# FFT filter and MLP on one Trainium2 core: first matmul two chunks ahead on a third PSUM bank, FFT steps in halves

## The chip, the cores and the metric

The kernel runs on 1 core of a Trainium2 chip. The metric is the device time in microseconds from start to end of one execution; several executions are made and their median counts.

## The reference

```python
X = np.fft.rfft(x, axis=1)                    # x: 8 images x 3008 tokens x 256
Y = X * (filt_r + 1j * filt_i)[None]
x = np.fft.irfft(Y, n=3008, axis=1).reshape(24064, 256)
h = x @ w_in                                  # 256 -> 2048
g = h * (1 / (1 + np.exp(-1.702 * h)))
out = g @ w_out                               # 2048 -> 256
```

All inputs are float32. The kernel gets the accuracy of float32 from pairs of matmuls on split numbers: a value is a high part (float32r) and a low part, and products of high x high, high x low and low x high are summed in PSUM.

## The kernel before, in words

**The work.** The 3008-point transform is split into 64 x 47 points. For each image (b = 0 to 7) it takes: stage one (64-point transforms over the rows of x, result a stored to DRAM as a_d), stage two (16 frequency groups: 47-point transform, product with the filter, inverse 47-point transform, result b stored to DRAM as b_d), and per tile of tokens the last inverse transform (`signal`, L626), which makes y. The MLP (`mlp`, L688) works on tiles of 512 tokens, six per image (384 for the sixth of an even image), 48 in all.

**The MLP.** A tile has 16 chunks of 128 hidden columns. `first(fc)` makes h with six matmuls (L701) into a bank of `ps_h` (two banks). ScalarE writes gh, the high part of the gelu (L704), and the gelu itself back into the bank (L705); VectorE subtracts and writes gl (L706), which frees the bank. `second(fc)` adds gh and gl times w_out into two banks of `ps_o` (L723), six matmuls; the two of gl are held over to the next chunk. The loop at the end of the program goes through all chunks: `ahead` calls `first` of chunk n + 1, then comes `second` of chunk n.

**The FFT beside it.** While the MLP works on image b, the generator `fft(b + 1)` (L448) makes the transform of the next image. It yields between steps. A planner in the main loop (L787, L808) gives each step a cost (`COSTS`, L25) and runs it when the tokens passed reach the matching share of `whole`:

```python
passed, whole = 0, sum(widths) - (40 if b else 26)
while steps and spent + steps[0] <= sum(COSTS[b]) * passed / whole + 0.01:
    run(nxt, 1)
```

For images 2 to 7 stage one is `packed` (L483): `fetch` loads x two blocks ahead (SP's queue), `butterfly` adds and subtracts on GpSimd (L504), `split` casts the high part on ScalarE or VectorE (L511) and subtracts on GpSimd (L512), `transform` (L514) does two matmuls (L521) into two banks of `ps_f` (four banks), casts the high parts (L526: h = 0 on ScalarE, h = 1 on VectorE) and on VectorE subtracts and adds (L527, L528). The two stores of each of the 12 transforms go into the list `late`; `keep` issues them from ScalarE's queue one step later (L453). Image 1 uses `thrice`, image 0 a function of its own ahead of the loop.

Stage two: `load` fetches from a_d by GpSimd's queue (L558), `forward` (L579) does the matmuls of both halves k into two banks (`second`, L569 to L574; tile s), merges them (`halves`, L442 on ScalarE, L443 on VectorE), multiplies with the filter (L433 to L436) and splits the product into y (tile zy, L590 on VectorE, L591 on GpSimd). `backward` (L597) transforms that back (tile i), merges it and stores b from ScalarE's queue (L606). Each forward step is followed by the backward step of the group before.

**What sets the order.** Tile's scheduler orders each engine's instructions by a forecast of its own, with program order as the priority, and may issue an instruction well ahead of its place in the program. `keep_in_program_order` pins an instruction behind what was traced on its engine before; the first matmul of each FFT step is pinned. Engines run their queues in order. `signal` of the next tile is started at the chunks in `at` (L811): loads of br, then the two halves of the last transform (L674, L682, L683).

Of the kernel before, what the change touches and what calls it, by code (L numbers as in the profile page):

```python
# [19 lines left out]
NH = 24  # L20
P = 128
Q = 112
NFC = DFF // P
LATER = [1.0, 1.4] + [1.25, 0.75] * 15 + [1.0]
COSTS = [[0.746] * 12 + [1.212] * 2 + LATER] + [[0.8] * 3 + [1.35] * 12 + [1.3] * 2 + LATER] * 7  # L25

# [132 lines left out]
def tile_kernel(  # L159
# [13 lines left out]
    dram1 = ctx.enter_context(tc.tile_pool(name="dram1", bufs=1, space=bass.MemoryType.DRAM))  # L173
    ps_f = ctx.enter_context(tc.tile_pool(name="ps_f", bufs=4, space=bass.MemoryType.PSUM))
    ps_h = ctx.enter_context(tc.tile_pool(name="ps_h", bufs=2, space=bass.MemoryType.PSUM))
# [5 lines left out]
    def half(name):  # L181
        return sb.tile([P, 2, D], F32R, tag="half", name=name, bufs=5)

    in_order = [True]
# [107 lines left out]
    def bank(name):  # L292

        pool, tag = banks[n_bank[0] % 4]
        n_bank[0] += 1
        return pool.tile([P, 2, D], F32, tag=tag, name=name)

# [139 lines left out]

    def halves(ps, dst):

        for k in range(2):  # L440
            h, o = slice(64 * k, 64 * k + 48), slice(64 - 64 * k, 112 - 64 * k)
            nc.scalar.copy(dst[h], ps[k][o])  # L442
            nc.vector.tensor_tensor(dst[h], ps[k][h], dst[h], ALU.add)  # L443

    def fft(b):
# [10 lines left out]
        def thrice():  # L456

            for c in range(6):
# [3 lines left out]
                for u in range(2):  # L462
                    xh, xl = half(f"xh_{b}_{c}_{u}"), half(f"xl_{b}_{c}_{u}")
                    src = xr[:, 2 * u : 2 * u + 2, :]
                    nc.scalar.copy(xh, src)
                    nc.gpsimd.tensor_tensor(xl, src, xh.bitcast(F32), ALU.subtract)
                    ps = ps_f.tile([P, 2, D], F32, tag="f", name=f"s1_{b}_{c}_{u}")
                    mm3(ps, t1_sb[0][:, 0], t1_sb[0][:, 1], xh, xl)
                    su = slice(2 * u, 2 * u + 2)
                    nc.scalar.copy(ah[:, su], ps)  # L470
                    nc.vector.tensor_tensor(al[:, su], ps, ah[:, su].bitcast(F32), ALU.subtract)
                    keep()
                    yield
# [9 lines left out]
        def packed():  # L483
# [21 lines left out]

            def split(n):
                if n < 12:
                    src = sums.pop(n)
                    es[n] = [half(f"e{h}_{b}_{n}") for h in range(2)]
                    for h, (t, o) in enumerate(sides):  # L510
                        (nc.vector.tensor_copy if h else nc.scalar.copy)(es[n][h][t], src[t])  # L511
                        nc.gpsimd.tensor_tensor(es[n][h][o], src[t], es[n][h][t].bitcast(F32), ALU.subtract)  # L512

            def transform(n):  # L514
                c, j = divmod(n, 2)
                a = sb.tile([P, 2, 2, D], F32, tag="raw", name=f"a_{b}_{n}", bufs=7)
                ps = [ps_f.tile([P, 2, D], F32, tag="f", name=f"s1_{b}_{n}_{h}") for h in range(2)]
                e = es.pop(n)
                for h in range(2):
                    w = t1_sb[1][:, h, j].rearrange("p a c -> p (a c)")  # L520
                    ins = nc.tensor.matmul(ps[h], w, e[h], start=True, stop=True)  # L521
                    if h == 0:
                        tc.keep_in_program_order(ins)
                for h, (t, o) in enumerate(sides):
                    hi, lo = a[t, 0].bitcast(F32R), a[t, 1]
                    (nc.vector.tensor_copy if h else nc.scalar.copy)(hi, ps[h][t])  # L526
                    nc.vector.tensor_tensor(lo, ps[h][t], a[t, 0], ALU.subtract)  # L527
                    nc.vector.tensor_tensor(lo.bitcast(F32R), lo, ps[h][o], ALU.add)  # L528
                    q = NH * j + 4 * c + 2 * h
                    to = a_d[:, :, q : q + 2].rearrange("k s n d -> s k n d")  # L530
                    late.append((to, a[t]))

            for c in range(2):
                fetch(c)
            yield
            butterfly(0)
            butterfly(1)
            yield
            split(0)
            yield  # L540
            for n in range(12):
                transform(n)
                split(n + 1)
                butterfly(n + 2)
                if n % 2 == 0:
                    fetch(n // 2 + 2)
                if n:
                    keep()
                yield

# [12 lines left out]

        def second(i, m, src, name):

            ps = [ps_f.tile([P, 2, D], F32, tag="f", name=f"{name}_{b}_{i}_{k}") for k in range(2)]
            for k in range(2):
                if i == 0:
                    ins = nc.tensor.matmul(ps[k][:, 0], de_sb[:, k, m + 1], src[:, k, 0], start=True, stop=True)  # L569
                    if k == 0:  # L570
                        tc.keep_in_program_order(ins)
                    nc.tensor.matmul(ps[k][:, 1], de_sb[:, k, m], src[:, k, 1], start=True, stop=True)
                else:
                    ins = nc.tensor.matmul(ps[k], de_sb[:, k, m], src[:, k], start=True, stop=True)  # L574
                    if k == 0:
                        tc.keep_in_program_order(ins)
            return ps

        def forward(i):  # L579

            ps = second(i, 0, zy[0][:, i % 2], "s2")
            if i + 2 < 16:
                load(i + 2)
            u1 = c_buf[i % 3]
            halves(ps, u1)
            product(i, u1, u1, f_buf[:Q, 2 * (i % 2) : 2 * (i % 2) + 2])
            y = zy[0][:, 2 + i % 2]
            for k in range(2):
                h, o = slice(64 * k, 64 * k + 48), slice(64 - 64 * k, 112 - 64 * k)
                nc.vector.tensor_copy(y[h, k], u1[h])  # L590
                nc.gpsimd.tensor_tensor(y[o, k], u1[h], y[h, k].bitcast(F32), ALU.subtract)  # L591
            if i + 2 < 16:
                load_f(i + 2)

        bes = {}

        def backward(i):  # L597
            g, u = divmod(i, 2)
            if u == 0:
                bes[g] = raw(f"b_{b}_{g}")  # L600
            ps = second(i, 2, zy[0][:, 2 + i % 2], "i2")
            halves(ps, bes[g][:Q, 2 * u : 2 * u + 2, :])
            if u == 1:
                be = bes.pop(g)
                for k in range(2):
                    nc.scalar.dma_start(b_d[:, 32 * k + 4 * g : 32 * k + 4 * g + 4, :], be[64 * k : 64 * k + 48])  # L606

# [9 lines left out]
        for i in range(17):  # L617
            if i < 16:
                forward(i)
                yield  # L620
            if i:
                backward(i - 1)
                yield
        b_of[b] = b_d

    def signal(b, t, y):  # L626
# [11 lines left out]
        def turn(m):  # L638

            ps = ps_f.tile([P, 4, P], F32, tag="f", name=f"bt_{t}_{m}")  # L640
            if t == m == 0:
# [25 lines left out]
        for m in range(2):  # L667
            if b == 0 and 1 not in br:
                br[1] = turn(1)
            ps = ps_f.tile([P, 512], F32, tag="f", name=f"i1_{b}_{t}_{m}")  # L670
            if b == t == m == 0:
# [15 lines left out]

    def mlp(b, t, y, nb, sums=(ps_o, "o")):  # L688

# [6 lines left out]
        def first(fc):  # L696
            ps = ps_h.tile([P, 512], F32, tag="h", name=f"h_{b}_{t}_{fc}")
            half, o = divmod(fc, HALF)
# [10 lines left out]
        def second(fc, hold):  # L709
            if fc == 0:  # L710
                pos.extend(sums[0].tile([P, 512], F32, tag=sums[1], name=f"o_{b}_{t}_{m}") for m in range(2))
            gp = gs.pop(fc)
# [61 lines left out]
    def ahead(i, fc):  # L774
        if i not in chunks_of:
            b, t = tiles[i]
            chunks_of[i] = mlp(b, t, ys.pop((b, t)), 4 if t < 5 or b % 2 else 3, (ps_f, "f") if i == 1 else (ps_o, "o"))
        chunks_of[i][0](fc)

    ahead(*turns[0])  # L780
    for n, (i, fc) in enumerate(turns):
        b, t = tiles[i]
        if n % (6 * NFC) == 0:

            lead = 16 if b == 0 else 0
            widths = [3 if k // NFC == 5 and b % 2 == 0 else 4 for k in range(lead, 6 * NFC)]
            passed, whole = 0, sum(widths) - (40 if b else 26)  # L787
            steps, spent = list(COSTS[b]), 0.0
            nxt = fft(b + 1) if b + 1 < B else iter(())
        if n == 0:  # L790
            run(start(*tiles[1]))
        if n + 1 < len(turns):
            ahead(*turns[n + 1])
        chunks_of[i][1](fc, turns[n + 1 : n + 2] == [(i, fc + 1)])
# [11 lines left out]
        if b or n >= lead:  # L806
            passed += widths.pop(0)
            while steps and spent + steps[0] <= sum(COSTS[b]) * passed / whole + 0.01:  # L808
                run(nxt, 1)
                spent += steps.pop(0)  # L810
        at = (9, 12, 13) if t == 5 else (1, 3, 9)  # L811
        if n in (23, 26, 27) or i > 1 and fc in at and i + 1 < len(tiles):
# [35 lines left out]
```

## Time and profile before

| | us |
|---|---|
| median of 3 runs | 2419.93 (2415.69 to 2422.02) |
| the profiled execution | 2423.5 |
| its span, first to last instruction | 2421.7 |

The rows below are of this one profiled execution. PE is TensorE's matmuls, PEld its weight loads, DVE VectorE, ACT ScalarE, POOL GpSimd, SP the queue of loads and output stores; "ACTq" is an instruction that ScalarE's sequencer issues. A number in square brackets at the end of a line of the timeline is the engine's idle time before it, and what ended it.

### The profile page before, as it was taken

How to read it: one execution, taken by the hardware profiler on the slowest of the kernel's cores; microseconds unless marked ns; L12 is line 12 of the kernel's file. 1: busy time of each engine (PE TensorE's matmuls, PEld its weight loads, DVE VectorE, ACT ScalarE, POOL GpSimd, SP SyncE). 2: the span in 40 equal slices, each digit the busy share in tenths (PEclk: the TensorE clock that was granted, in tenths of full speed). 3: DMA queues.
4: the chain of work that ended last, by engine and by line, in shares of the span. 5: the costliest groups of instructions: out<-in, count | busy, mean ns of one | idle time of the engine just before them, and what ended most of it. 6: DMA issues, size and time to landing. Idle time of an engine off the chain costs nothing. (4 is left out here: it accounts for less than half of the span.)

```text
span 2421.7 us, 31798 instructions
## 1 busy us (share of the span) xinstructions
PE 2371.3 (98%) x11030; PEld 1973.8 (82%) x11030; DVE 1653.3 (68%) x2561; ACT 1305.8 (54%) x2431; POOL 918.0 (38%) x819
## 2 busy tenths in 40 slices
PE   9999999999999999999999999999999999999999
PEld 7878897788777888788877788878887788898887
DVE  7968857788477883878848788387883878822222
ACT  6666655466444664456644466445664456644443
POOL 3035534355343552535525355253542535500000
PEclk9999999999999999999999999999999999999999
DMA  8265433455334552345524454244542445320000
GB/s 330 87 184 113 109 107 96 100 116 116 83 109 100 123 118 84 99 105 119 116 86 104 105 129 110 74 111 105 119 114 74 118 104 126 96 65 9 18 9 18
DMA packets 139952, 248.77 MB, mean 103 GB/s; under 512 B 15376, under 2 KB 81040, under 8 KB 139792
## 3 DMA queue, kind: packets, MB, share of 16 engines
q1 hardware_dynamic: 63088, 136.25, 19.2%
q0 software_dynamic: 46592, 44.05, 10.7%
q10 hardware_dynamic: 30112, 66.44, 10.6%
q8 instruction: 88, 1.44, 0.2%
q14 instruction: 72, 0.59, 0.1%
HBM read 152.83 MB, written 93.85 MB: 102 GB/s over the span
## 5 line engine op out<-in xcount | busy, mean ns | idle before, releaser
L701 PE MATMUL h<-y,wi 128*128 128x512 f32 (+1 forms) x4608 | 1172.8, 390 | 24.0 <-DVE gl L706 23.8
L701 PEld LDWEIGHTS h<-y,wi 128*128 128x128 f32 x4608 | 854.1, 189 | 202.4 <-DVE gl L706 44.5
L706 DVE TENSOR_TENSOR gl<-h,gh 128x512 fp32r<-128x512 f32 (+1 forms) x768 | 522.4, 680 | 571.6 <-ACT h L705 561.2
L704 ACT ACTIVATE gh<-h 128x512 fp32r<-128x512 f32 (+1 forms) x768 | 452.9, 590 | 819.4 <-PE h L701 625.6
L723 PE MATMUL o<-gh,wo 128*128 128x512 f32 (+1 forms) x3072 | 821.1, 387 | 14.7 <-ACT gh L704 14.7
L723 PEld LDWEIGHTS o<-gh,wo 128*128 128x128 f32 x3072 | 573.6, 189 | 127.9 <-ACT gh L704 18.9
L723 PE MATMUL o<-gl,wo 128*128 128x512 f32 (+1 forms) x1536 | 476.7, 387 | 3.2 <-DVE gl L706 3.2
L705 ACT ACTIVATE h<-h 128x512 f32<-128x512 f32 (+1 forms) x768 | 448.3, 584 | 0.0
L591 POOL TENSOR_TENSOR zy<-c_buf,zy 48x512 fp32r<-48x512 f32 x224 | 315.2, 1407 | 74.7 <-DVE zy L590 66.0
L723 PEld LDWEIGHTS o<-gl,wo 128*128 128x128 f32 x1536 | 288.7, 189 | 60.7 <-DVE gl L706 5.3
L436 POOL TENSOR_TENSOR c_buf<-c_buf,u_buf 112x512 f32<-112x512 f32 x127 | 163.9, 1290 | 388.4 <-DVE c_buf L435 388.4
L558 POOL DMA_DIRECT2D zy<-a_d x224 | 130.6, 588 | 223.8 <-DMA a_d<-a 113.5
L512 POOL TENSOR_TENSOR e<-ev,e 64x512 fp32r<-64x512 f32 x72 | 96.7, 1343 | 246.8 <-ACT e L511 228.3
L443 DVE TENSOR_TENSOR c_buf<-s,c_buf 48x512 f32<-48x512 f32 x224 | 154.3, 689 | 33.6 <-ACT c_buf L442 29.3
L443 DVE TENSOR_TENSOR b<-i,b 48x512 f32<-48x512 f32 x224 | 154.1, 688 | 15.0 <-ACT b L442 9.6
L442 ACT COPY c_buf<-s 48x512 f32<-48x512 f32 x224 | 130.3, 582 | 51.0 <-PE s L574 30.9
L442 ACT COPY b<-i 48x512 f32<-48x512 f32 x224 | 130.2, 581 | 48.6 <-PE i L574 42.1
L512 POOL TENSOR_TENSOR e<-x,e 64x512 fp32r<-64x512 f32 x72 | 92.8, 1289 | 64.5 <-ACT e L511 47.5
L590 DVE CAST zy<-c_buf 48x512 fp32r<-48x512 f32 x224 | 94.6, 422 | 32.9 <-POOL c_buf L436 26.9
L674 PEld LDWEIGHTS i<-tab,br 128*128 128x128 f32 x752 | 100.9, 191 | 8.8 <-PE s L521 1.2
L674 PE MATMUL i<-tab,br 128*128 128x128 f32 x752 | 103.0, 275 | 0.1
L527 DVE TENSOR_TENSOR a<-s,a 64x512 f32<-64x512 f32 x144 | 99.2, 689 | 4.4
(113 smaller groups left out, 1483.4 us busy)
## 6 DMA issues: line engine op xcount, KB each, us to landing
f_buf<-fs SPq DMA_DIRECT2D x224, 192.0 KB, 3.1
zy<-a_d POOLq DMA_DIRECT2D x224, 192.0 KB, 3.6
a_d<-a ACTq DMA_DIRECT2D x144, 256.0 KB, 3.1
x<-in_x_dram SPq DMA_DIRECT2D x47, 512.0 KB, 5.1
out_dram<-out SPq DMA_DIRECT2D x43, 512.0 KB, 3.9
b_d<-b ACTq DMA_DIRECT2D x112, 192.0 KB, 2.5
br<-b_d SPq DMA_DIRECT2D x84, 256.0 KB, 4.6
f_y<-in_filt_dram SPq DMA_DIRECT2D x8, 512.0 KB, 8.3
```

Source lines behind the costliest of these rows:

```text
L436: eng.tensor_tensor(u1, u1, u2, ALU.add)
L442: nc.scalar.copy(dst[h], ps[k][o])
L443: nc.vector.tensor_tensor(dst[h], ps[k][h], dst[h], ALU.add)
L512: nc.gpsimd.tensor_tensor(es[n][h][o], src[t], es[n][h][t].bitcast(F32), ALU.subtract)
L558: nc.gpsimd.dma_start(zy[0][64 * k : 64 * k + 48, i % 2].rearrange("p k s d -> p (k s) d"), src)
L591: nc.gpsimd.tensor_tensor(y[o, k], u1[h], y[h, k].bitcast(F32), ALU.subtract)
L674: ins = nc.tensor.matmul(ps[:, P * i : P * i + P], br[m][:, i], t2_sb, start=True, stop=True)
L701: nc.tensor.matmul(ps[:, :w], wi_sb[half][:, wk, kc, c], y[:, yk, kc, :w], start=n == 0, stop=n == 5)
L704: nc.scalar.activation(gh[:, :w], ps[:, :w], AF.Gelu_apprx_sigmoid)
L705: nc.scalar.activation(ps[:, :w], ps[:, :w], AF.Gelu_apprx_sigmoid)
L706: nc.vector.tensor_tensor(gl[:, :w], ps[:, :w], gh[:, :w].bitcast(F32), ALU.subtract)
L723: ins = nc.tensor.matmul(pos[m][:, :w], wb[:, P * m : P * m + P], g[:, :w], start=first_one, stop=last_one)
```

## The change

`ps_f` has three banks, and one bank `ps_x` is lent out by a new function `ring`. For images 1 to 7 it is the third bank of h. `first` runs two chunks ahead of `second` there. The functions `transform`, `split`, `forward` and `backward` do one half (h or k) per step with one bank; both high casts of `transform` are on ScalarE. A store is issued when more than two are in the list. There is one more empty step between the first fetch and the butterflies. The costs follow; `whole` is less by 48 instead of 40; `at` is earlier for images 1 to 7. The product of `forward` begins with half 0 while half 1 is still to come. Arithmetic and the number of instructions of each kind stay, apart from the engine of 72 casts. The core of the diff:

```diff
-LATER = [1.0, 1.4] + [1.25, 0.75] * 15 + [1.0]
-COSTS = [[0.746] * 12 + [1.212] * 2 + LATER] + [[0.8] * 3 + [1.35] * 12 + [1.3] * 2 + LATER] * 7
+LATER = [0.5, 0.5, 1.0, 0.4] + [0.625, 0.625, 0.375, 0.375] * 15 + [1.0]
+COSTS = [[0.746] * 12 + [1.212] * 2 + LATER] + [[0.8] * 4 + [0.675] * 24 + [1.3] * 2 + LATER] * 7
...
-    ps_f = ctx.enter_context(tc.tile_pool(name="ps_f", bufs=4, space=bass.MemoryType.PSUM))
+    ps_f = ctx.enter_context(tc.tile_pool(name="ps_f", bufs=3, space=bass.MemoryType.PSUM))
+    ps_x = ctx.enter_context(tc.tile_pool(name="ps_x", bufs=1, space=bass.MemoryType.PSUM))
...
+    shared, turn_of = ["f"], {"f": 0, "h": 0}
+
+    def ring(kind, shape, name):
+
+        own = {"f": (ps_f, 3), "h": (ps_h, 2)}[kind]
+        turn_of[kind] += 1
+        if shared[0] == kind and turn_of[kind] % (own[1] + 1) == 0:
+            return ps_x.tile(shape, F32, tag="x", name=name)
+        return own[0].tile(shape, F32, tag=kind, name=name)
...
+            def transform(n, h):
                 c, j = divmod(n, 2)
...
+                ps = ring("f", [P, 2, D], f"s1_{b}_{n}_{h}")
+                w = t1_sb[1][:, h, j].rearrange("p a c -> p (a c)")
+                tc.keep_in_program_order(nc.tensor.matmul(ps, w, es.pop((n, h)), start=True, stop=True))
+                hi, lo = a[t, 0].bitcast(F32R), a[t, 1]
+                nc.scalar.copy(hi, ps[t])
+                nc.vector.tensor_tensor(lo, ps[t], a[t, 0], ALU.subtract)
+                nc.vector.tensor_tensor(lo.bitcast(F32R), lo, ps[o], ALU.add)
...
             for c in range(2):
                 fetch(c)
-            yield
+            for c in range(2):
+                yield
...
             for n in range(12):
-                transform(n)
-                split(n + 1)
-                butterfly(n + 2)
-                if n % 2 == 0:
-                    fetch(n // 2 + 2)
-                if n:
-                    keep()
-                yield
+                for h in range(2):
+                    transform(n, h)
+                    split(n + 1, h)
+                    if h:
+                        butterfly(n + 2)
+                        if n % 2 == 0:
+                            fetch(n // 2 + 2)
+                    if len(late) > 2:
+                        keep(1)
+                    yield
...
+            u1, u2 = c_buf[i % 3], u_buf[i % 2]
...
+            merge(0, second(i, 0, zy[0][:, i % 2], "s2", 0), u1)
+            nc.vector.tensor_tensor(u2[64:Q], u1[0:48], f_i[0:48], ALU.mult)
+            yield
+            merge(1, second(i, 0, zy[0][:, i % 2], "s2", 1), u1)
             if i + 2 < 16:
                 load(i + 2)
...
+            for k in range(2):
+                merge(k, second(i, 2, zy[0][:, 2 + i % 2], "i2", k), bes[g][:Q, 2 * u : 2 * u + 2, :])
...
+                yield
...
-            passed, whole = 0, sum(widths) - (40 if b else 26)
+            passed, whole = 0, sum(widths) - (48 if b else 26)
...
+        if n == 2 * NFC:
+            shared[0] = "f"
+        if n == 6 * NFC:
+            shared[0] = "h"
+        while begun <= min(n + 1 + (n >= 6 * NFC), len(turns) - 1):
+            ahead(*turns[begun])
+            begun += 1
...
-        at = (9, 12, 13) if t == 5 else (1, 3, 9)
+        at = (1, 3, 6) if t < 5 and b else (1, 3, 9) if t < 5 else (8, 11, 12) if b else (9, 12, 13)
```

## Rows read from the trace of the kernel before

**Rows 1.** The page, part 1: busy time, share of the span, instructions.
```profile
PE 2371.3 (98%) x11030; PEld 1973.8 (82%) x11030; DVE 1653.3 (68%) x2561; ACT 1305.8 (54%) x2431; POOL 918.0 (38%) x819
```
**Rows 2.** Windows: length, busy PE, PEld, DVE, ACT, POOL, clock, DMA share, GB/s.
```profile
676.00:768.00 92.00, 87.98 (x386) 69.51 (x385) 73.19 (x104) 44.44 (x85) 38.88 (x32) 1.00 0.45 112
768.00:915.00 147.00, 147.00 (x680) 122.87 (x679) 124.25 (x199) 91.14 (x165) 79.33 (x75) 1.00 0.50 114
```
**Rows 3.** Waits of PEld, whole run: us in total, times, longest us.
```profile
PEld h L701 <- DVE gl L706: 44.5, 53, 1.8
PEld o L723 <- ACT gh L704: 18.9, 12, 3.6
...
PEld o L723 <- DVE gl L706: 5.3, 5, 1.3
```
**Rows 4.** Timeline, 700 to 703 us: start, us, engine, line, operation.
```profile
700.21 1.40 DVE L528 TENSOR_TENSOR a<-a,s 64x512 fp32r<-64x512 f32 x2
...
700.98 1.24 ACTq L453 DMA_DIRECT2D a_d<-a  x2
...
702.27 0.60 ACT L704 ACTIVATE gh<-h 128x512 fp32r<-128x512 f32 x1 [3.63 <-PE s L521]
702.38 1.23 PEld L701 LDWEIGHTS h<-y,wi 128*128 128x128 f32 x6 [0.76 <-DVE gl L706]
702.38 1.65 PE L701 MATMUL h<-y,wi 128*128 128x512 f32 x6 [0.33 <-DVE gl L706]
```
**Rows 5.** Waits of PEld, 376 to 470 us (stage one of image 2).
```profile
PEld h L701 <- DVE gl L706: 6.0, 5, 1.7
```
**Rows 6.** Waits of PEld, 676 to 770 us (stage one of image 3).
```profile
PEld h L701 <- DVE gl L706: 6.9, 10, 1.8
```
**Rows 7.** Waits of PEld, 625 to 662 us (the boundary after image 1).
```profile
PEld o L723 <- ACT gh L704: 3.6, 1, 3.6
```
**Rows 8.** Timeline, 630 to 641 us.
```profile
630.30 1.07 SPq L188 DMA_DIRECT2D x<-in_x_dram  x2
...
639.03 0.62 ACT L511 CAST e<-ev 64x512 fp32r<-64x512 f32 x1 [6.76 <-POOL ev L504]
...
639.55 0.58 ACT L704 ACTIVATE gh<-h 128x512 fp32r<-128x512 f32 x1
640.04 0.58 ACT L705 ACTIVATE h<-h 128x512 f32<-128x512 f32 x1
640.19 1.36 PEld L723 LDWEIGHTS o<-gh,wo 128*128 128x128 f32 x4 [3.63 <-ACT gh L704]
```
**Rows 9.** The window 640 to 650 us, columns as in rows 2.
```profile
640.00:650.00 10.00, 9.81 (x34) 7.91 (x35) 3.09 (x5) 4.38 (x9) 8.50 (x7) 0.70 0.00 0
```
**Rows 10.** The core's span and mean granted TensorE clock.
```profile
core 0: 2421.7 us, clock 0.995
```
**Rows 11.** Groups by form: count, busy us, mean ns, idle before.
```profile
L706 DVE TENSOR_TENSOR gl<-h,gh 128x512 fp32r<-128x512 f32 x704 | 486.7, 691 | 512.6 <-ACT h L705 503.2
...
L526 DVE CAST a<-s 64x512 fp32r<-64x512 f32 x72 | 50.0, 695 | 2.2
...
L526 ACT CAST a<-s 64x512 fp32r<-64x512 f32 x72 | 41.8, 580 | 20.3 <-DVE a L528 9.1 <-PE s L521 8.0 <-issue 2.8
```
**Rows 12.** Timeline, 450 to 466 us: last transform to first forward step.
```profile
450.18 0.62 PE L521 MATMUL s<-e,t_two 128*128 128x512 f32 x2
...
458.79 2.30 POOL L558 DMA_DIRECT2D zy<-a_d  x4 [18.83 <-DMA a_d<-a]
...
465.17 0.36 PE L569 MATMUL s<-zy,de_sb 128*128 128x256 f32 x1 [0.77 <-DMA zy<-a_d]
```
**Rows 13.** Timeline, 494 to 511 us: one forward step, its y, its backward step.
```profile
494.02 0.62 PE L574 MATMUL s<-zy,de_sb 128*128 128x512 f32 x2
...
501.25 2.88 POOL L591 TENSOR_TENSOR zy<-c_buf,zy 48x512 fp32r<-48x512 f32 x2 [0.53 <-DVE zy L590]
...
510.56 0.62 PE L574 MATMUL i<-zy,de_sb 128*128 128x512 f32 x2
```

More of the change, by code (lines that the diff above doesn't have):

```diff
@@ L295, in bank @@
         n_bank[0] += 1
+        if tag == "f":
+            return ring("f", [P, 2, D], name)
         return pool.tile([P, 2, D], F32, tag=tag, name=name)
@@ L436, in product @@
         eng.tensor_tensor(u1, u1, u2, ALU.add)
[L438 to L443, printed above, removed]
     def fft(b):
@@ L466, in thrice @@
                     nc.gpsimd.tensor_tensor(xl, src, xh.bitcast(F32), ALU.subtract)
-                    ps = ps_f.tile([P, 2, D], F32, tag="f", name=f"s1_{b}_{c}_{u}")
+                    ps = ring("f", [P, 2, D], f"s1_{b}_{c}_{u}")
                     mm3(ps, t1_sb[0][:, 0], t1_sb[0][:, 1], xh, xl)
@@ L504, in butterfly, with split @@
                     nc.gpsimd.tensor_tensor(sums[n], xs[c][:, 0], xs[c][:, 1], ALU.subtract if j else ALU.add)
-            def split(n):
+            def split(n, h):
                 if n < 12:
[L508 to L512, printed above, removed]
@@ L514, in transform @@
-            def transform(n):
-                c, j = divmod(n, 2)
[L516 to L531, printed above, removed]
+                    src, (t, o) = sums[n], sides[h]
@@ new lines, in split @@
+                    es[n, h] = half(f"e{h}_{b}_{n}")
+                    (nc.vector.tensor_copy if h else nc.scalar.copy)(es[n, h][t], src[t])
+                    nc.gpsimd.tensor_tensor(es[n, h][o], src[t], es[n, h][t].bitcast(F32), ALU.subtract)
+            made = {}
+            def transform(n, h):
+                c, j = divmod(n, 2)
+                if h == 0:
+                    made[n] = sb.tile([P, 2, 2, D], F32, tag="raw", name=f"a_{b}_{n}", bufs=7)
+                a, (t, o) = made[n], sides[h]
+                ps = ring("f", [P, 2, D], f"s1_{b}_{n}_{h}")
[5 more added lines that the diff above has]
+                nc.vector.tensor_tensor(lo.bitcast(F32R), lo, ps[o], ALU.add)
+                q = NH * j + 4 * c + 2 * h
+                late.append((a_d[:, :, q : q + 2].rearrange("k s n d -> s k n d"), a[t]))
@@ L538, in packed @@
             yield
-            split(0)
+            for h in range(2):
+                split(0, h)
             yield
             for n in range(12):
-                transform(n)
-                split(n + 1)
-                butterfly(n + 2)
-                if n % 2 == 0:
-                    fetch(n // 2 + 2)
-                if n:
-                    keep()
-                yield
+                for h in range(2):
+                    transform(n, h)
[7 more added lines that the diff above has]
+                    yield
         yield from packed() if b > 1 else thrice()
@@ L562, in load_f @@
                 load_in(f_buf[64 * k : 64 * k + 48, 2 * (i % 2) : 2 * (i % 2) + 2], fs[i])
[L564 to L576, printed above, removed]
-            return ps
@@ L579, in forward, with second @@
-        def forward(i):
-            ps = second(i, 0, zy[0][:, i % 2], "s2")
+        def second(i, m, src, name, k):
+            pin = tc.keep_in_program_order
+            ps = ring("f", [P, 2, D], f"{name}_{b}_{i}_{k}")
+            if i == 0:
+                pin(nc.tensor.matmul(ps[:, 0], de_sb[:, k, m + 1], src[:, k, 0], start=True, stop=True))
+                nc.tensor.matmul(ps[:, 1], de_sb[:, k, m], src[:, k, 1], start=True, stop=True)
+            else:
+                pin(nc.tensor.matmul(ps, de_sb[:, k, m], src[:, k], start=True, stop=True))
+            return ps
@@ new lines, in sides, with merge @@
+        def sides(k):
+            return slice(64 * k, 64 * k + 48), slice(64 - 64 * k, 112 - 64 * k)
+        def merge(k, ps, dst):
+            h, o = sides(k)
+            nc.scalar.copy(dst[h], ps[o])
+            nc.vector.tensor_tensor(dst[h], ps[h], dst[h], ALU.add)
+        def forward(i):
+            u1, u2 = c_buf[i % 3], u_buf[i % 2]
+            fr = f_buf[:Q, 2 * (i % 2) : 2 * (i % 2) + 2]
+            f_r, f_i = fr[:, :, 0, :], fr[:, :, 1, :]
+            merge(0, second(i, 0, zy[0][:, i % 2], "s2", 0), u1)
+            nc.vector.tensor_tensor(u2[64:Q], u1[0:48], f_i[0:48], ALU.mult)
+            yield
+            merge(1, second(i, 0, zy[0][:, i % 2], "s2", 1), u1)
@@ L582, in forward @@
             if i + 2 < 16:
                 load(i + 2)
-            u1 = c_buf[i % 3]
-            halves(ps, u1)
-            product(i, u1, u1, f_buf[:Q, 2 * (i % 2) : 2 * (i % 2) + 2])
+            nc.vector.scalar_tensor_tensor(u2[0:48], u1[64:Q], -1.0, f_i[64:Q], ALU.mult, ALU.mult)
+            nc.vector.tensor_tensor(u1, u1[:Q], f_r, ALU.mult)
+            nc.gpsimd.tensor_tensor(u1, u1, u2, ALU.add)
             y = zy[0][:, 2 + i % 2]
             for k in range(2):
-                h, o = slice(64 * k, 64 * k + 48), slice(64 - 64 * k, 112 - 64 * k)
+                h, o = sides(k)
@@ L600, in backward @@
                 bes[g] = raw(f"b_{b}_{g}")
[L601 to L606, printed above, removed]
+            for k in range(2):
+                merge(k, second(i, 2, zy[0][:, 2 + i % 2], "i2", k), bes[g][:Q, 2 * u : 2 * u + 2, :])
+                if k and u:
+                    be = bes.pop(g)
+                    for n in range(2):
+                        nc.scalar.dma_start(b_d[:, 32 * n + 4 * g : 32 * n + 4 * g + 4, :], be[64 * n : 64 * n + 48])
+                yield
         keep(4)
@@ L618, in fft @@
             if i < 16:
-                forward(i)
-                yield
+                yield from forward(i)
             if i:
-                backward(i - 1)
-                yield
+                yield from backward(i - 1)
         b_of[b] = b_d
@@ L638, in turn @@
         def turn(m):
-            ps = ps_f.tile([P, 4, P], F32, tag="f", name=f"bt_{t}_{m}")
+            ps = ring("f", [P, 4, P], f"bt_{t}_{m}")
             if t == m == 0:
@@ L669, in signal @@
                 br[1] = turn(1)
-            ps = ps_f.tile([P, 512], F32, tag="f", name=f"i1_{b}_{t}_{m}")
+            ps = ring("f", [P, 512], f"i1_{b}_{t}_{m}")
             if b == t == m == 0:
@@ L686, in signal, with mlp @@
             yield
-    def mlp(b, t, y, nb, sums=(ps_o, "o")):
+    def mlp(b, t, y, nb, sums):
         w = P * nb
@@ L696, in first @@
         def first(fc):
-            ps = ps_h.tile([P, 512], F32, tag="h", name=f"h_{b}_{t}_{fc}")
+            ps = ring("h", [P, 512], f"h_{b}_{t}_{fc}")
             half, o = divmod(fc, HALF)
@@ L710, in second @@
             if fc == 0:
-                pos.extend(sums[0].tile([P, 512], F32, tag=sums[1], name=f"o_{b}_{t}_{m}") for m in range(2))
+                pos.extend(p.tile([P, 512], F32, tag=k, name=f"o_{b}_{t}_{m}") for m, (p, k) in enumerate(sums))
+                if sums[0][0] is ps_x:
+                    shared[0] = None
             gp = gs.pop(fc)
@@ L776, in ahead @@
             b, t = tiles[i]
-            chunks_of[i] = mlp(b, t, ys.pop((b, t)), 4 if t < 5 or b % 2 else 3, (ps_f, "f") if i == 1 else (ps_o, "o"))
+            chunks_of[i] = mlp(b, t, ys.pop((b, t)), 4 if t < 5 or b % 2 else 3, [(ps_x, "x"), (ps_f, "f")] if i == 1 else [(ps_o, "o")] * 2)
         chunks_of[i][0](fc)
     ahead(*turns[0])
+    begun = 1
     for n, (i, fc) in enumerate(turns):
@@ L791, in tile_kernel @@
             run(start(*tiles[1]))
-        if n + 1 < len(turns):
-            ahead(*turns[n + 1])
+        if n == 2 * NFC:
[5 more added lines that the diff above has]
+            begun += 1
         chunks_of[i][1](fc, turns[n + 1 : n + 2] == [(i, fc + 1)])
```

## The prediction

> **What bounds the kernel now.** I read the page's busy table first: TensorE's matmuls are busy 98% of the span, its weight loads 82% [rows 1]. The 98% says little, because a matmul's record is longer than the interval between two starts. The windows say what a full TensorE looks like: from 768 to 915 us (stage two) it has no idle time, and 679 loads fill 122.87 of 147 us, one every 0.216 us. From 676 to 768 us (stage one) it has 385 loads in 92 us and idles [rows 2]. So the kernel runs at TensorE's pace, less stalls that sit in certain places, and the question is how much stall there is and which of it the change reaches.
>
> The Trainium skill (Trainium Kernel Development and Optimization, Performance Expectations) calls matmul busy time a bad metric and wants weight-load busy time instead. Taken as a share of 100%, that would leave 18%, an estimated 448 us, to gain. The trace disagrees: a stretch without any gap stands at 122.87/147 = 83.6%.
>
> Against that 83.6%, the run's 1973.8 us of loads would need 2361 us, so some 60 us are in hand, not 448. The view of waits says where. Weight loads waited 44.5 us for gl (VectorE), 18.9 for gh (ScalarE) and 5.3 for gl again: 68.7 us in 70 waits [rows 3]. Each counts about 0.2 us too much: behind a stall a load and its matmul start together (702.38 in [rows 4]), otherwise the load goes ahead by one beat. So 70 x 0.2 = 14 off: **55 us of stall**.
>
> They lie in two kinds of place. **Stage one** (six times, for images 2 to 7): 5 waits of 6.0 us in one, 10 of 6.9 in the next [rows 5, 6], alternating, some others beside them: about 33 us of the 55 after the correction. One of them, in [rows 4]: two L528 subtractions on VectorE, behind them the two stores that ScalarE issues (it stands in its own queue until VectorE is through), then gh 3.63 us late, then TensorE. **The boundary**, five times, shortly before an image ends: the next image's x was asked for at 630.30, and ScalarE, which holds the cast of it in its queue, waits 6.76 us; gh is late and TensorE stops 3.63 us [rows 7, 8]. About 17 us in all. The remaining 5 us lie in the first image.
>
> Each boundary stop is followed by a slower clock: granted 0.70 over the 10 us from 640 [rows 9], that is, part of it at 1.2 GHz instead of 2.4. Over the run the mean grant is 0.995 [rows 10]: 0.005 x 2421.7 = **12 us**.
>
> **The change, part by part.** *h two chunks ahead, third bank.* Now gh(n) must be ready when TensorE has done o(n-1) and h(n+1) after h(n); with the change another h and another o lie between: 12 matmuls x 0.216 = 2.6 us more room, for gl's release of the bank as well. Chunks of 384 columns give about 2.0. Matmul work is the same. Every wait of stage one is at most 1.8 us [rows 3, 5, 6], below 2.6. At the boundary 3.6 - 0.2 - 2.6 = 0.8 remains at the longest. The stall must not build up from chunk to chunk, which leads to the next item. Price in bounds: all 50 us of images 1 to 7 gone, or none if the wait is one of throughput.
>
> *Split steps, both hi casts on ScalarE.* Per old step of 1.35 units the planner passes 1.35 x 86/54.6 = 2.13 chunks, 27.5 matmuls, 6.0 us. VectorE has 6 operations of the step (one is the hi cast, 0.695) and 2.13 gl at 0.691 [rows 11], taking 0.69 for all: 5.6 of 6.0 us, 94%. That is why it is late. After: two half steps, 1.35 x 84/55.4 = 2.05 chunks, 26.6 matmuls, 5.75 us; VectorE 5 x 0.69 + 1.41 = 4.9, 85%. ScalarE takes the 72 casts at 0.58. Its operations start 0.49 us apart when back to back (639.55 and 640.04 [rows 8]), two stores cost 1.24 [rows 4]: 3 x 0.5 + 1.24 + 4.1 x 0.5 = 4.8 of 5.75, 83%; with the full 0.58 or so each, 93%. Neither is over 100%, so I take the stalls as covered, with 4 of 33 us left. Both ends: 0 and 33.
>
> *Stores later, loads sooner.* In [rows 4] the stores block ScalarE because they wait for L528. They are listed one half step later, but the scheduler issues by its own forecast, so I give them nothing; cover as above. Queued behind a store on ScalarE are gh and h. The signal's second part goes from chunk 9 to 6, br's load at the end from 9 to 8: SP's queue holds x, br, f_buf and output stores, and nothing of it is late in stage two [rows 2]. The empty step between fetch and butterfly gives x 0.8 units more by program order; the cast was hoisted some eight chunks before its place anyway [rows 8], so I count it at nothing and let ScalarE's 6.76 us stay. Boundary: 17 us, of which 3 stay; clock: 12 us, of which 2 stay, since stage one, stalls up to 1.8 us included, has a grant of 1.00 [rows 2, 6].
>
> *The first forward step comes sooner.* From the last transform to it the planner now passes 3.6 units x 1.575 = 5.67 chunks, 15.0 us from 450.18 to 465.17, and there TensorE already waits 0.77 us for the zy load [rows 12]. New: 3.1 x 1.516 = 4.70 chunks, 12.4 us. The chain (subtract, store, landing, GpSimd's load at 458.79, landing) shortens by two or three VectorE operations, to about 13.3. That gives a wait of some 1 us, six times, on a pinned matmul that no third bank covers. Bounds 0 and 2.6 each, 0 to 16; taken: 4 us more than now.
>
> *Stage two in halves, one bank each of three.* Same operations. From a forward step to the backward step that uses it: 16.54 us now (494.02 to 510.56), y done 10.1 us after the first (501.25 + 2.88) [rows 13]. New: 2.625 units x 1.516 against 3.25 x 1.575, 78%: 12.9 us. 2.8 us of margin stay. Nothing.
>
> **Sum.** 33 - 4 + 17 - 3 + 12 - 2 - 4 = 49, call it 50. The profiled execution took 2423.5 us, 3.6 over the median of 2419.93. 2423.5 - 50 - 3.6 = **2370 us**.
>
> **Rivals.**
> *A, all of it.* Every stall is covered and the first forward step costs nothing: another 13 us and the short stalls that no view lists: 2350 to 2357. For it: no wait in stage one exceeds the new room. Against: the zy load's 0.77 us.
> *B, ScalarE takes VectorE's place.* Stage one's gh is late as gl was, because 0.58 us casts and stores that wait share a queue at 83 to 93%: the 30 us stay, 2400. For it: [rows 4], where ScalarE is already the one blocked. Against: it starts an operation every 0.5 us.
> *C, it does not do what it says.* The instruction order is the scheduler's; if it puts h(n+2) behind o(n), only VectorE's 72 x 0.69 = 50 us of work moved counts, perhaps a third of stage one's stalls less the 4 us: 2412.
> *D, slower.* Stage two's beat is too tight: the backward matmul, pinned, waits for GpSimd's y at 16 x 6 = 96 places. It decides when y comes later than 12.9 us after its forward step. One us late at each is 96 us, so 2370 + 96 = 2466. For it: 2.8 us of margin, rounded to whole chunks. Against: the k=0 half is merged ahead, and the first backward half needs only the first of y's two subtractions.
>
> **How the numbers follow.** Forecast 0.60, A 0.12, B 0.13, C 0.08, D 0.07. Within 0.3% (7 us, about what a measurement of this kernel can tell from no change) lies half of C and a little of B: 0.06. Slower: D, 0.07. Faster: 0.87. The range from A's lower end to B's takes 0.85: 2350 to 2402.
>
> **What would show it.** Right: waits of weight loads for L706 and L704 fall from 68.7 to under 20 us and the granted clock goes to 1.00, with ScalarE still waiting some 6 us for x at the boundary; VectorE's share of stage one falls; L569 waits for DMA in most images. Wrong: gh waits in stage one (B), h not ahead of o in the order (C), gaps in stage two before L574 or L569 (D).

## The result and the profile after

The changed kernel takes 2360.84 us (median of 4 runs, 2359.94 to 2362.96) against 2417.81 for the kernel before on the same chips: a ratio of 0.976, 95% interval 0.975 to 0.978. The forecast was 2370, range 2350 to 2402. The profiled execution took 2360.66 us, its span is 2358.8.

The page, part 1, and the waits of the weight loads over the whole run, as in [rows 1] and [rows 3]:

```profile
PE 2344.1 (99%) x11030; PEld 1970.9 (84%) x11030; DVE 1625.4 (69%) x2489; ACT 1351.1 (57%) x2503; POOL 917.5 (39%) x819
```
```profile
...
PEld h L718 <- DVE gl L723: 6.4, 6, 1.5
PEld o L742 <- ACT gh L721: 5.0, 4, 2.3
PEld o L742 <- DVE gl L723: 1.5, 2, 1.0
...
PEld s L576 <- issue: 0.5, 1, 0.5
```

12.9 us of waits for gl and gh are left of 68.7, and 12 waits of 70. The line left out at the top is a wait in the transform of image 0, ahead of the MLP: 9.1 us, against 9.2 before. Loads and matmuls are as many as before. The core's granted clock and the windows of stage one and stage two of image 3, as in [rows 10] and [rows 2]:

```profile
core 0: 2358.8 us, clock 1.000
```
```profile
676.00:752.00 76.00, 76.00 (x345) 63.26 (x344) 56.02 (x81) 45.17 (x83) 34.34 (x29) 1.00 0.56 128
752.00:908.00 156.00, 154.88 (x728) 130.99 (x727) 133.95 (x201) 95.76 (x176) 79.02 (x74) 1.00 0.49 110
```

Stage one has no gap left. The 0.005 of clock is back too in this execution; the four executions have 0.998 to 1.000. At the boundary after image 1 ScalarE still waits for x, but for 3.60 us instead of 6.76 [rows 8], and TensorE does not notice. Over the six boundaries this wait of ScalarE is 21.6 us instead of 32.0. The timeline there:

```profile
630.61 1.07 SPq L199 DMA_DIRECT2D x<-in_x_dram  x2
...
634.22 0.59 ACT L722 ACTIVATE h<-h 128x512 f32<-128x512 f32 x1
...
638.41 0.62 ACT L516 CAST e<-ev 64x512 fp32r<-64x512 f32 x1 [3.60 <-POOL ev L510]
```
```profile
640.00:650.00 10.00, 10.00 (x50) 8.43 (x49) 3.88 (x7) 6.00 (x12) 7.94 (x6) 1.00 0.01 2
```

The window from 640 to 650 us stands at 1.00 where [rows 9] had 0.70. What is new is a small wait at the end of each image whose last tile has 384 columns, three times (it ends at 906, 1482 and 2058 us). The timeline of the first:

```profile
901.22 3.16 POOL L608 TENSOR_TENSOR zy<-c_buf,zy 48x512 fp32r<-48x512 f32 x2 [1.78 <-PE o L742]
...
901.56 1.66 DVE L596 TENSOR_TENSOR u_buf<-c_buf,f_buf 48x512 f32<-48x512 f32 x1
...
903.25 1.67 DVE L601 SCALAR_TENSOR_TENSOR u_buf<-c_buf,f_buf 48x512 f32<-48x512 f32 x1
...
905.57 1.00 PEld L718 LDWEIGHTS h<-y,wi 128*128 128x128 f32 x6 [1.50 <-DVE gl L723]
```

The two products on VectorE take 1.66 us each while GpSimd runs L608; gl stands behind them.

The wait for gh at the end of image 0 has grown, from 0.78 us in the kernel before (first line) to 2.28 us (second line):

```profile
348.44 0.64 PEld L723 LDWEIGHTS o<-gh,wo 128*128 128x128 f32 x4 [0.78 <-ACT gh L704]
```
```profile
347.61 0.64 PEld L742 LDWEIGHTS o<-gh,wo 128*128 128x128 f32 x4 [2.28 <-ACT gh L721]
```

### The profile page after: what moved, and what is told of

Read it like the earlier page. It is cut to its first block, busy times and chain, and to the rows that moved or that the text cites. A ratio compares the mean times of both kernels' runs of the same rounds, so it can differ in the third digit from the quotient of the medians.

```text
span 2358.8 us, 32215 instructions
## 1 busy us (share of the span) xinstructions
PE 2344.1 (99%) x11030; PEld 1970.9 (84%) x11030; DVE 1625.4 (69%) x2489; ACT 1351.1 (57%) x2503; POOL 917.5 (39%) x819
## 4 chain that ended last, share of the span: by engine, by line
PE 90%; DVE 1%; DMA 1%; issue 0%; ACT 0%; POOL 0%; SPq 0%; ACTq 0%; POOLq 0%
PE o L742 40%; PE h L718 40%; PE i L691 3%; PE s L579 2%; PE i L579 2%; PE s L528 1%; DVE u_buf L601 0%; DMA x<-in_x_dram 0%; DMA br<-b_d 0%; DVE gl L723 0%; DVE u_buf L596 0%; DMA b_d<-b 0%; DVE zy L607 0%; SPq L199 0%; DVE b L588 0%
## 5 line engine op out<-in xcount | busy, mean ns | idle before, releaser
L718 PE MATMUL h<-y,wi 128*128 128x512 f32 (+1 forms) x4608 | 1188.3, 387 | 4.3 <-DVE gl L723 3.8
L742 PE MATMUL o<-gh,wo 128*128 128x512 f32 (+1 forms) x3072 | 839.6, 385 | 3.6 <-ACT gh L721 3.6
L742 PE MATMUL o<-gl,wo 128*128 128x512 f32 (+1 forms) x1536 | 484.1, 385 | 0.6 <-DVE gl L723 0.6
L608 POOL TENSOR_TENSOR zy<-c_buf,zy 48x512 fp32r<-48x512 f32 x224 | 316.8, 1414 | 80.9 <-DVE zy L607 64.6
L603 POOL TENSOR_TENSOR c_buf<-c_buf,u_buf 112x512 f32<-112x512 f32 x112 | 144.5, 1290 | 314.8 <-DVE c_buf L602 314.7
L607 DVE CAST zy<-c_buf 48x512 fp32r<-48x512 f32 x224 | 100.5, 449 | 29.5 <-POOL c_buf L603 23.9
L530 ACT CAST a<-s 64x512 fp32r<-64x512 f32 x144 | 83.7, 581 | 62.0 <-PE s L528 38.3
L596 DVE TENSOR_TENSOR u_buf<-c_buf,f_buf 48x512 f32<-48x512 f32 x112 | 106.5, 951 | 3.8
```

The costliest lines, as they stand in the source:

```text
L596: nc.vector.tensor_tensor(u2[64:Q], u1[0:48], f_i[0:48], ALU.mult)
L603: nc.gpsimd.tensor_tensor(u1, u1, u2, ALU.add)
L718: nc.tensor.matmul(ps[:, :w], wi_sb[half][:, wk, kc, c], y[:, yk, kc, :w], start=n == 0, stop=n == 5)
L742: ins = nc.tensor.matmul(pos[m][:, :w], wb[:, P * m : P * m + P], g[:, :w], start=first_one, stop=last_one)
```

## The experiments

Each ran against the kernel before on its own chip: 2416.88 us for the first four, 2422.23 for the next four, 2419.68 for the last four. So the ratios compare better than the times.

**The bank without the distance.**
```diff
-        while begun <= min(n + 1 + (n >= 6 * NFC), len(turns) - 1):
+        while begun <= min(n + 1, len(turns) - 1):
```


> The changed kernel with the third bank still lent to h, but h only one chunk ahead of o, as before. Theory: the distance covers the waits for gh, the bank those for gl's release. The bank alone then cures stage one, where TensorE waited for the bank (44.5 us of waits for gl), but not the boundaries, where it waited for gh: about 17 us of stall and 12 us of clock come back, less what the smaller ScalarE wait there (3.6 us instead of 6.8) saves; 2370 to 2385. Rival 1, the split steps did it all: 2361. Rival 2, the distance did it all: 2400 or more.


Measured: 2362.86 us, ratio 0.9775 (0.9759 to 0.9791). The changed kernel stands at 0.9764. Nothing beyond the noise came back: rival 1 as far as this run goes, and the theory's 9 us or more are refuted.

**The half steps without bank and distance.** As the run above, and without
```diff
-        if n == 6 * NFC:
-            shared[0] = "h"
```


> The changed kernel without third bank and distance: f has its four banks again, h two, h one chunk ahead; the half steps, casts on ScalarE, stores and loads as changed. Theory: the room for gh and gl is what counts; the half steps alone take VectorE from 94 to 85% and remove perhaps half of stage one's 33 us of stall, while the boundaries keep most of 17 + 12 us: 2385 to 2405. Rival, the relief of VectorE did it: under 2370.


Measured: 2373.70 us, 0.9823 (0.9809 to 0.9838), clock 0.997. Between the two: the steps alone bring 1.8 of the 2.4%. Its waits:
```profile
PEld o L742 <- ACT gh L721: 12.4, 9, 3.3
...
PEld h L718 <- DVE gl L723: 6.4, 8, 1.0
```
No weight load waits for gl or gh from 370 to 470 or from 676 to 760 us, so stage one is cured without any bank. Nor does any gh of ScalarE wait for VectorE's a in this run (48.5 us in 16 waits before). What is left lies at the ends of images: 3.3 us for gh after image 0, and at the five boundaries 7.0 us for gh and 4.5 for gl.

**The bank and the distance without the half steps.** The kernel before with `ring`, `ps_x` and `begun` of the diff, and nothing else of it.


> The kernel before with nothing but h two chunks ahead on a third bank (f has three, and its old steps still take two at a time). Theory: every wait of stage one was at most 1.8 us, below the 2.6 us of new room, so stage one is cured although VectorE stays at 94%; the boundary keeps 0.8 us; 2362 to 2375. Rival, VectorE's load decides, and the third bank that f lost makes the transforms wait: 2390 to 2410.


Measured: 2359.22 us, 0.9763 (0.9749 to 0.9778). The theory holds: all of the gain without the steps. Half of the waits on ScalarE's queue are still there, and TensorE has no gap beside them (waits of ScalarE before and in this run, and this run's window in image 3's stage one, 690 to 740 us):
```profile
ACT gh L704 <- DVE a L528: 48.5, 16, 4.6
```
```profile
ACT gh L717 <- DVE a L541: 26.5, 12, 4.4
```
```profile
690.00:740.00 50.00, 50.00 (x230) 41.73 (x229) 43.41 (x66) 25.35 (x49) 20.57 (x16) 1.00 0.49 124
```

**One cast back on VectorE.**
```diff
-                nc.scalar.copy(hi, ps[t])
+                (nc.vector.tensor_copy if h else nc.scalar.copy)(hi, ps[t])
```


> The changed kernel with the high cast of half 1 on VectorE again (72 casts of 0.695 us back). VectorE's operations then fill 6 x 0.69 + 1.41 = 5.6 of 5.75 us of a step in stage one, 97%. Theory: below 100% the room of one chunk covers it: 2360 to 2366. Rival, the casts' move to ScalarE was the cure of stage one: 2375 to 2395.


Measured: 2360.44 us, 0.9767 (0.9752 to 0.9781). The move of the casts is worth nothing here.

**Both casts on VectorE.** The same line with `nc.vector.tensor_copy` alone.


> The changed kernel with both high casts of a transform on VectorE (144 of 0.695 us, none on ScalarE). By the prediction's sum VectorE then needs 7 x 0.69 + 1.41 = 6.2 us in each step of 5.75 us: 108%, over twelve steps 5.9 us too much per image. Theory, room covers lateness but not a load over 100%: the first 2.6 us of it are hidden, about 3 us per image come back as waits for gl, six times: 2375 to 2385. Rival, the room covers this too: 2361 to 2365.


Measured: 2360.66 us, 0.9748 (0.9726 to 0.9769). The rival's time, but not for its reason: the load is not over 100%. The window from 690 to 740 us:
```profile
690.00:740.00 50.00, 50.00 (x231) 41.67 (x230) 47.55 (x73) 22.89 (x43) 25.47 (x20) 1.00 0.47 120
```
VectorE is busy 95%, and TensorE has no gap. The 108% took 0.69 us for the cast of the split, which is shorter on VectorE (medians of 425 ns where it reads ev, 450 where it reads x), and a step's time without the matmuls of the last transform. So whether a load over 100% could be covered was not tried.

**Stores at once.**
```diff
-                    if len(late) > 2:
+                    if late:
                         keep(1)
```


> The changed kernel with the store of a half step listed for issue in that very step, not when more than two are waiting. Theory: the scheduler issues a store when it takes its data to be ready, so the list changes little: 2359 to 2364, with ScalarE's queue waiting on VectorE's subtraction in a few places. Rival, a later store is what keeps ScalarE's queue free: gh is late in stage one and the time goes to 2370 or more.


Measured: 2362.73 us, 0.9757 (0.9739 to 0.9775). As the theory has it: when a store is listed makes no difference.

**The old pacing.** One `yield` behind the first fetch, 0.8 three times, 40 instead of 48, the old `at`.


> The changed kernel with the old pacing: no empty step behind the first fetch, the image's work spread to 40 instead of 48 before the end, signals at the old chunks. Theory: ScalarE's wait for x at the boundary goes back from 3.6 to some 6 us, of which the room covers all but 0.8 us: 2361 to 2368, clock 0.998 or better. Rival, the pacing cured the boundary: 17 us of stall and 12 us of clock come back in part, 2375 or more.


Measured: 2356.99 us, 0.9735 (0.9717 to 0.9752). Below what the theory gave: the boundaries need no new pacing, and the waits at the ends of images of 384 columns are gone. Repeated below.

**The bank in image 0 too.** `shared[0] = "h"` and the distance from `n == 2 * NFC` on.


> The changed kernel with the third bank and the distance of two chunks from the third tile on, that is, in image 0 too. Left there are a wait of 2.3 us for gh at the end of image 0 and one of 0.6 us near 188 us. Theory: they go as the others did: 2358 to 2360, 2 to 3 us less. Rival, image 0's stage one wants the fourth bank of f: 2361 or more.


Measured: 2362.15 us, 0.9757 (0.9738 to 0.9776). No gain, which is the rival's side, but its reason is not shown: the time can't be told from the changed kernel's. The wait of 2.3 us for gh at the end of image 0 is gone, and at 351 and 357 us others have taken its place, for the last transform (i) and for y:
```profile
PEld h L718 <- DVE y L700: 4.2, 3, 3.2
PEld i L691 <- issue: 2.0, 1, 2.0
```

**Old steps, bank, no distance.** The third run with h one chunk ahead.


> The kernel before with the third bank lent to h but h still one chunk ahead: the run with h two ahead (2359) less the distance. Theory: the bank gives gl's release one chunk more, so stage one's waits for gl (44.5 of 68.7 us) go; gh is needed as early as before, so the boundaries keep about 17 us and the clock its 12 us, less what the bank lets TensorE run on: 2375 to 2390, clock 0.996 to 0.998. Rival 1, the bank is the whole cure and the scheduler makes the distance itself: 2359 to 2364. Rival 2, without the distance the bank is worth nothing: 2410 or more.


Measured: 2356.86 us, 0.9738 (0.9721 to 0.9754), clock 1.000: rival 1's side, below its range, and with the first run of the old pacing the lowest time of all. The waits that the bank was put there for are gone, at the boundaries too:
```profile
PEld o L738 <- ACT gh L717: 6.1, 6, 1.8
PEld h L714 <- DVE gl L719: 1.4, 4, 0.5
```
The scheduler does make part of the distance. Counted in the order of TensorE's records, for the 656 chunks n from 96 to 751, by how many chunks of h are through ahead of o(n), h(n) among them:

```
                               2     3     4     5
before                       639    17
old steps, bank, no distance 378   240    38
changed kernel                 9   583    46    18
```

With the bank free, o(n) is overtaken by h(n + 2) in 278 of the 656 chunks, presumably where the scheduler's forecast has gh or gl late; the forecast itself is not on record. The timeline of a stretch of its stage one, 696.7 to 700 us: 14 matmuls of h (12 make two chunks) with one of stage one between them and none of o, and no gap on TensorE.
```profile
696.73 1.29 PE L714 MATMUL h<-y,wi 128*128 128x512 f32 x5
...
697.87 0.39 PE L534 MATMUL s<-e,t_two 128*128 128x512 f32 x1
...
698.09 2.20 PE L714 MATMUL h<-y,wi 128*128 128x512 f32 x9
...
698.97 0.59 ACT L717 ACTIVATE gh<-h 128x512 fp32r<-128x512 f32 x1
```

**Half steps alone, cast on VectorE.** The second and the fourth edit together.


> The run of the half steps alone (2374: no third bank, one chunk ahead) with the high cast of half 1 on VectorE again. Theory: the halves themselves cured stage one there, because gl stands behind three of a step's VectorE operations instead of six; the cast moves only 50 us of work: 2372 to 2380, waits for gl under 15 us. Rival, what cured it was VectorE's load, lower by one operation in six: waits for gl come back, 2385 to 2400.


Measured: 2372.85 us, 0.9802 (0.9787 to 0.9817); waits for gl 6.4 and 1.2 us, none of them in stage one of images 2 and 3. The theory's side: VectorE's load is not what the steps cured.

**Old pacing and changed kernel on one chip.**


> The changed kernel with the old pacing once more (2357 in its first run), beside the changed kernel on the same chip. Theory: the tighter pacing costs some 3 us, so it is again 2 to 5 us below the changed kernel. Rival: the difference was the chip's, within 1 us.


Measured: 2360.99 us (2357.85 to 2363.29), 0.9753 (0.9738 to 0.9768).


> The changed kernel itself, beside the old pacing on one chip: 2360 to 2362, with TensorE waiting 1.5 us for gl at the end of the images of 384 columns, three times.


Measured: 2362.75 us, 0.9761 (0.9746 to 0.9775), 6.4 us of waits for gl as before. 1.8 us lie between the two and the runs overlap, so the pacing is not decided. The wait for gh at the end of image 0 is 3.98 us in this profile, and over the ten us from 345 TensorE is granted 0.66 (part of it 1.2 GHz, first line) where the first profile of the same kernel has 1.00 (second line):
```profile
345.00:355.00 10.00, 6.43 (x28) 6.43 (x29) 2.66 (x5) 3.34 (x7) 8.32 (x7) 0.66 0.16 36
```
```profile
345.00:355.00 10.00, 8.04 (x55) 7.72 (x54) 3.90 (x7) 5.23 (x12) 9.29 (x7) 1.00 0.28 53
```
The old steps with the bank are 5.9 us below the changed kernel on this chip. The intervals of the two ratios overlap by 0.0008, since both hold the spread of the kernel before; the runs themselves do not overlap, 2356.25 to 2357.62 against 2361.50 to 2363.93. So on this chip, with the bank in place, the rest of the change costs time; on the first chip the old steps with bank and distance lay only 1 to 4 us below the two variants of the changed kernel, with runs that overlap. The traces of this chip show where: 1.5 us at the end of three images against 1.0 at two of them, and 3.98 us against 1.80 at the end of image 0.

## Why the prediction was right, point by point

**The bound** held: the gain is the stalls' 55 us and the clock's 12 us, less what is left. The medians differ by 2417.81 - 2360.84 = 57 us. The sum's 50 is of the profiled execution, though, and the two spans differ by 2421.7 - 2358.8 = 62.9: 58 waits with 55.8 us fewer, less 0.2 us each, are 44, the clock's 12 make 56, the waits ahead of the first forward step (3.0 us) 59; the last 4 lie in no wait that was followed. The sum fell short because what it kept back was not needed: 4 us in stage one, 3 at the boundaries, 2 of clock and 4 for the first forward step.

**The room of one chunk** held in size, and its cause was put too narrowly. I gave it to the distance in program order; the bank alone does it, with the old steps and with the new, because the order is the scheduler's. That was the point of rival C, and it came out the other way round: what is not written down happens all the same. In the changed kernel, where the distance is written down, h is three or more chunks through in 647 of 656 places, so C did not come. Stage one had 4 us left in the sum and has none.

**Split steps and casts** is the step that failed in its reasoning, not in the time. The 94% of VectorE was too high (43.31 of 50 us are 87% in the kernel before, and 81% after, from 690 to 740 us):
```profile
690.00:740.00 50.00, 47.14 (x203) 36.47 (x202) 43.31 (x61) 25.40 (x49) 27.38 (x21) 1.00 0.51 132
```
```profile
690.00:740.00 50.00, 50.00 (x230) 41.73 (x229) 40.51 (x60) 31.64 (x59) 22.87 (x18) 1.00 0.53 128
```
Nor was it why gl was late: at 95% with both casts and the bank there is no wait, and the half steps cure stage one with or without the cast. What the runs leave is this reading: TensorE waits when gl, or a gh in a blocked ScalarE queue, is behind a burst of VectorE's work for longer than the room. That the time came out all the same is luck in this point, since the bank was part of the same change and is enough by itself. Either a shorter burst or more room cures stage one, so the two parts do not add up: steps alone 43 us (2416.88 - 2373.70), bank and distance alone 58, the bank alone 63 (2419.68 - 2356.86), all together 57 on two sets of chips. Whether the shorter burst comes from the halves or from the stores and pacing that went with them was not separated; with the bank, no gain of the latter two was measured.

**Stores and loads at nothing** held, within the resolution. ScalarE's wait at the boundary did not stay at 6.76 us; it is 3.60 us after image 1. So this sign of being right did not come, nor did waits of L569 for DMA in most images; the fall of VectorE's share of stage one did, from 80 to 74% in the windows of image 3.

**The first forward step** was mis-sized: 4 us more were taken, and 3.0 us less were measured. The kernel before waited there in three of the six images (at 465, 1065 and 1664 us), the changed kernel in none; the 0.5 us of L576 above lie at 178 us, in image 0. The timeline after, to be held against [rows 12]:
```profile
448.64 0.39 PE L528 MATMUL s<-e,t_two 128*128 128x512 f32 x1
...
455.41 2.29 POOL L565 DMA_DIRECT2D zy<-a_d  x4 [16.04 <-DMA a_d<-a]
...
463.37 0.28 PE L576 MATMUL s<-zy,de_sb 128*128 128x256 f32 x1
```
From the last transform to the load it is 6.8 us instead of 8.6, the shortening that was forecast. The step itself came after 14.7 us, not after 12.4, and in the other images after 14.5 or 14.7. That is late enough for the load, and it is why the wait did not come. Why the step was no earlier is open: the planner rounds to whole chunks, five here in both kernels, but four for image 3, where it still came after 14.5 us.

**Stage two** (rival D) held: TensorE waits there only in the three places with 384 columns above. **Rival B** did not show: gh is on time in stage one although ScalarE has the casts.

**A** was the nearest of the rivals, with 2350 to 2357. The changed kernel is 4 us above it. Its 4.5 us of waits at the ends of images of 384 columns and 2.3 us at the end of image 0 would account for that, but this is not shown: the run without the former was not decided, and the run without the latter gained nothing.

## What to carry to other kernels

Where an engine at full pace waits for the release of a buffer in many small waits, none longer than one more buffer would cover, try the buffer first and alone: here one PSUM bank, taken from the four of the FFT, which did without it, brought all of the gain, and on one chip more than the whole change. Cures of the same wait do not add up, so take parts back one at a time before keeping all of them. And an order written into the program is a wish where a scheduler has the last word; a free buffer is what lets it act.

## What was not expected of the hardware

VectorE's products of 48 partitions vary. The tile u_buf in the changed kernel (instruction and count, duration in ns: shortest, median, longest):
```profile
L596 DVE TENSOR_TENSOR u_buf<-c_buf,f_buf x112: 684/853/1722, 182.1 to 2053.8; 48x512 f32<-48x512 f32 x112
L601 DVE SCALAR_TENSOR_TENSOR u_buf<-c_buf,f_buf x112: 686/687/1769, 182.8 to 2055.5; 48x512 f32<-48x512 f32 x112
```
In the kernel before the median of the first was 685, at the same shape. In the trace of the changed kernel, all 74 of these 224 that took over 0.70 us overlap an operation of GpSimd on tiles, 71 of them L608; of the other 150 two do. In image 0, 30 products of the same shape that read one operand from PSUM (tile s) overlap GpSimd's L449, and none took over 0.70 us. So the long ones go with both operands in SBUF and GpSimd at work beside them. That GpSimd lengthens them was not tried by itself.
